# Where dense work stands between attention tiles: a gated linear-attention and ReLU block with split exponentials and a two-step key mask

## The chip, the cores and the metric

The kernel runs on one core of a Trainium2 chip. The metric is the device time of one execution in microseconds (us), as the median of several runs. The core has a matrix engine (PE, with a separate row PEld for its weight loads), a vector engine (DVE), an activation engine (ACT), GpSimd (POOL), and DMA queues, of which this kernel uses mostly that of SyncE (SP). Each engine works through its own list in order, and the lists are tied together by semaphores. PE writes its results to PSUM, which has eight banks; a bank can be written again only after ACT or DVE has read it.

## The reference, cut to what matters

```python
g = sigmoid((x * gate_w).sum(-1))                    # x: 2048 x 512, bf16
q, k, v = split(x @ wqkv)                            # 32 heads of 16
pq, pk = q @ w_phi, k @ w_phi                        # per head, 16 x 16
phi = concat([softmax(p), softmax(-p)])              # for pq and pk: 32 features
kv = einsum("bhsf,bhsd->bhfd", phi_k, v)             # sum over all 2048 rows
z  = einsum("bhsf->bhf", phi_k)
o  = (phi_q @ kv) / (phi_q . z + 1e-6)
a  = o @ wo
b  = relu(x @ w1) @ w2                               # hidden width 1376
out = g * a + (1 - g) * b
```

Two things follow for the order of work. Nothing of `o` can be computed before `kv` has been summed over all rows. And `relu(x @ w1)`, the dense branch, depends on nothing of the attention, so it can be placed anywhere.

## The kernel before, in words

The 2048 rows are 16 tiles of 128 (index m), and also 4 chunks of 512 (index c). A small planner class keeps a list per engine; `p.op(engine, fn, after, ev)` appends an instruction that waits for the events in `after` and signals `ev`. So the order of the calls is the order on each engine, and it is written out by hand at the end of the program (L477 to L573).

The attention work for tile m:

- `atile(m)` (L302): eight matmuls of 128x480 (L307), alternating between bank 0 (query) and bank 1 (key), give the head projections. Softmax is invariant to a shift, so 15 columns per head are computed and the sixteenth exponential is a constant 1. Then ACT makes two exponentials over both banks together (L318, 128x960 each): `ep`, with scale +1, and `em`, with scale -1. The banks are free for tile m+1 when `em` is done. DVE sums the key exponentials per head (L322, event `zk`), takes the reciprocal (L325, `rz`), sums the query's (L327, `zq`) and takes a reciprocal (L332, `rq`). POOL scales the key features (L334, `pk`), forms the query's factor (L339, `sc`) and scales half of the query features (L341, `pq`). A DMA transposes the query features into PHQ (L346, `tq`).
- `vtile(m)` (L350): four matmuls for the values in bank 2 (L354), copied out by ACT (L364).
- `kv(m)` (L367): eight matmuls of 128x65 (L376) that add the tile to the sums in banks 6 and 7; it waits for `pk` of tile m.
- `kvfin` (L382), after the last `kv`: DVE masks the sums to the block diagonal, one bank at a time: L385 and L389 for bank 6 (event `kvz0`), then for bank 7 (`kvz1`).
- `nd(m)` (L404): eight matmuls of 128x68 (L408) with KVNZ give numerator and denominator for tile m, four into each of two banks; even tiles use banks 0 and 1, odd ones 2 and 3. DVE takes the reciprocal (L414) and multiplies (L418, `om`), and a DMA transposes the result.

The dense branch: a *dense unit* `hunit(c, k)` (L254) is four matmuls of 128x512 (L257) in one of the banks 3 to 5 in rotation, and a ReLU on ACT (L243). A *ragged unit* `rest(c)` (L264) is sixteen narrow matmuls (L269) for the last 96 columns of the hidden width and the gate's column; ACT then makes a ReLU (L276) and the gate's exponential (L278). `finB(m)` (L429, matmuls at L433) is the second dense matmul of a tile, `finA(m)` (L440, L442) the output projection of the attention, and `comb(m)` (L452) mixes them (L456) and stores them. `gate()` (L397) is three small DVE instructions (L398, L400, L401) that turn the gate's exponentials into g and 1 - g.

The middle of the program is the loop over m at L523: `atile(m)`, `kv(m - 3)` from m = 3 on, `vtile(m + 3)` up to m = 12, and then units from the list `mid` (L511), dealt by a formula (L529). The formula gives:

```
m      0 1 2 | 3 4 5 6    7 8 9 10 11 12   13   14 15
dense  2 2 2 | 1 2 1 1    2 1 2 1  2  1    0    2  2
ragged       |       1                1    1
```

What stands on PE between `atile(m)` and `atile(m+1)` is called the *filler* below. After the loop come `gate()`, and the six units (3, 4) to (3, 9) of the list `late`, two after each of `kv(13)`, `kv(14)` and `kv(15)`; `kvfin` is queued on DVE after `kv(15)` (L542 to L551). Then `nd(0)`, `finB(0)`, `nd(1)` and the loop at L556. It runs `finB(1)`, `nd(2)`, `nd(3)`, `finA(0)` for m = 0, and then `nd(m + 3)`, `finB(m + 1)`, `finA(m)` for each further m.

Of the kernel before, what the change touches and what calls it, by code (L numbers as in the profile page):

```python
# [5 lines left out]
ACT = mybir.ActivationFunctionType  # L6
# [51 lines left out]
def bass_gated_mix__linear_kernel_hedgehog__dense_activation_relu__prompt_kernel(  # L58
# [13 lines left out]
    S, D = x2.shape  # L72
    H = A_w_phi.shape[0]
    DH = A_w_phi.shape[1]
    DFF = B_w1.shape[1]
    P = 128
    NT = S // P
    NDT = D // P
# [4 lines left out]
    NG = 8  # L83
    HG = H // NG
    FE = DH - 1
    DE = H * FE
    GW = 128
    NB = 5
    VB = 6
    LAG = 3  # L90
    KU = KT - 1
    NR = DFF - KU * P

    with ExitStack() as es:
        E = es.enter_context
        XT = E(nc.sbuf_tensor("XT", [P, NDT, S], BF16))
# [4 lines left out]
        WQK = E(nc.sbuf_tensor("WQK", [P, 2, NDT * D], BF16))  # L101
# [4 lines left out]
        EB = E(nc.sbuf_tensor("EB", [P, NB, 4, 2 * D], BF16))  # L106
# [22 lines left out]
        PS = E(nc.psum_tensor("PS", [P, 8, 512], FP32))  # L129
# [6 lines left out]
        EBS = NB * 4 * 2 * D  # L136
# [62 lines left out]
        def xready(c):  # L199
            return ["xa0", "xa1", "xa2", "xb1", "xb2"] if c == 0 else [f"x{c}"]  # L200
# [84 lines left out]
        def pre(i):  # L285
# [13 lines left out]
                     after=[f"pm{i}"], ev=f"pc{i}")  # L299
            free[bank] = [f"pc{i}"]  # L300

        def atile(m):  # L302
            b = m % NB
            first = xready(m // 4) + free[0] + free[1] + ([f"pc{i}" for i in range(8)] if m == 0 else [])
            for dt in range(NDT):
                for which in range(2):
                    p.op("pe", lambda e, dt=dt, which=which: e.matmul(  # L307
                        PS[:, which, 0:DE], XT[:, dt, m * P:(m + 1) * P], WQK[:, which, dt * DE:(dt + 1) * DE],
                        start=(dt == 0), stop=(dt == NDT - 1)),
                        after=(first if dt == 0 and which == 0 else ()),  # L310
                        ev=(f"qk{m}" if dt == NDT - 1 and which == 1 else None))
            src = PS[:, 0:2, 0:DE].rearrange("p a (h f) -> p a h f", h=H)
            base = b * 8 * D
            dsts = (bass.AP(tensor=EB, offset=base, ap=[[EBS, P], [4 * D, 2], [32, H], [1, FE]]),
                    bass.AP(tensor=EB, offset=base + 2 * D + 16, ap=[[EBS, P], [2 * D, 2], [32, H], [1, FE]]))
            busy = [f"tq{m - NB}", f"pk{m - NB}", f"pq{m - NB}"] if m >= NB else []
            for s, nm in ((0, "ep"), (1, "em")):
                p.op("act", lambda e, s=s, o=dsts[s]: e.activation(  # L318
                    o, src, ACT.Exp, scale=(1.0 if s == 0 else -1.0)),
                    after=[f"qk{m}"] + busy, ev=f"{nm}{m}")  # L320
            free[0] = free[1] = [f"em{m}"]
            p.op("dve", lambda e: e.tensor_reduce(  # L322
                ZB[:, b, 64:128], EB[:, b, 2, :].rearrange("p (g f) -> p g f", f=DH), AX.X, ALU.add),
                after=[f"em{m}", f"cst{b}"], ev=f"zk{m}")
            p.op("dve", lambda e: e.reciprocal(SC[:, b, 64:128], ZB[:, b, 64:128]),  # L325
                 after=[f"zk{m}"] + ([f"pk{m - NB}"] if m >= NB else []), ev=f"rz{m}")
            p.op("dve", lambda e: e.tensor_reduce(  # L327
                ZB[:, b, 0:64].rearrange("p (h s) -> p h s", s=2),
                bass.AP(tensor=EB, offset=base, ap=[[EBS, P], [32, H], [2 * D + 16, 2], [1, DH]]), AX.X, ALU.add),
                after=([f"sc{m - NB}"] if m >= NB else []), ev=f"zq{m}")  # L330
            zq = ZB[:, b, 0:64].rearrange("p (h s) -> p h s", s=2)
            p.op("dve", lambda e: e.reciprocal(SC[:, b, 32:64], zq[:, :, 1]),  # L332
                 after=[f"zq{m}"] + ([f"sc{m - NB}"] if m >= NB else []), ev=f"rq{m}")
            p.op("pool", lambda e: e.tensor_tensor(  # L334
                EB[:, b, 3, :].rearrange("p (g f) -> p g f", f=DH),
                EB[:, b, 2, :].rearrange("p (g f) -> p g f", f=DH),
                SC[:, b, 64:128].unsqueeze(2).to_broadcast([P, 2 * H, DH]), ALU.mult),
                after=[f"rz{m}"] + ([f"kv{m - NB}"] if m >= NB else []), ev=f"pk{m}")
            p.op("pool", lambda e: e.tensor_tensor(SC[:, b, 0:32], zq[:, :, 0], SC[:, b, 32:64], ALU.mult),  # L339
                 after=[f"rq{m}"], ev=f"sc{m}")  # L340
            p.op("pool", lambda e: e.tensor_tensor(  # L341
                EB[:, b, 0, :].rearrange("p (h s f) -> p h s f", h=H, s=2)[:, :, 1, :],
                EB[:, b, 1, :].rearrange("p (h s f) -> p h s f", h=H, s=2)[:, :, 1, :],
                SC[:, b, 0:32].unsqueeze(2).to_broadcast([P, H, DH]), ALU.mult),
                after=[f"sc{m}"] + ([f"tq{m - NB}"] if m >= NB else []), ev=f"pq{m}")
            p.dma("sp", lambda e: e.dma_start_transpose(  # L346
                out=PHQ[:, :, m * P:(m + 1) * P], in_=EB[:, b, 0, :]),
                f"tq{b}", after=[f"pq{m}", f"cst{b}"] + (["pm7"] if m == 12 else []), ev=f"tq{m}")
# [54 lines left out]

        def nd(m):  # L404
            b0 = 2 * (m % 2)
            after = [f"tq{m}", "kvz1"] + free[b0] + free[b0 + 1]
            for g in range(NG):
                p.op("pe", lambda e, g=g: e.matmul(  # L408
                    PS[:, b0 + g // 4, (g % 4) * GW:(g % 4) * GW + 68],
                    PHQ[:, g, m * P:(m + 1) * P], KVNZ[:, g, :], start=True, stop=True),  # L410
                    after=(after if g == 0 else ()), ev=(f"nd{m}" if g == NG - 1 else None))
            r = m % 2
            ob = m % 3
            p.op("dve", lambda e: e.reciprocal(  # L414
                RDEN[:, r, :].rearrange("p (g h) -> p g h", g=NG),
                bass.AP(tensor=PS, offset=b0 * 512 + 64, ap=[[EPS, P], [GW, NG], [1, HG]])),
                after=[f"nd{m}"], ev=f"rd{m}")
            p.op("dve", lambda e: e.tensor_tensor(  # L418
                OTM[:, ob, :].rearrange("p (g h d) -> p g h d", g=NG, h=HG),
                bass.AP(tensor=PS, offset=b0 * 512, ap=[[EPS, P], [GW, NG], [DH, HG], [1, DH]]),  # L420
                bass.AP(tensor=RDEN, offset=r * H, ap=[[2 * H, P], [HG, NG], [1, HG], [0, DH]]), ALU.mult),
                after=[f"rd{m}"] + ([f"to{m - 3}"] if m >= 3 else []), ev=f"om{m}")
            free[b0] = free[b0 + 1] = [f"om{m}"]
            p.dma("sp", lambda e: e.dma_start_transpose(
                out=OT[:, :, m * P:(m + 1) * P], in_=OTM[:, ob, :]), f"to{ob}", after=[f"om{m}"], ev=f"to{m}")
# [82 lines left out]
        for i in range(4, 8):  # L508
            pre(i)
        vtile(2, "dve")  # L510
        mid = [(1, k) for k in range(KU)] + [(1, -1)] + [(2, k) for k in range(KU)] + [(2, -1), (3, -1)]  # L511
        last = [(3, k) for k in range(KU)]
        mid += last[:4]
        late = last[4:]

        def unit(c, k):
            if k < 0:
                rest(c)
            else:
                hunit(c, k)  # L520

        done = 0
        for m in range(NT):  # L523
            atile(m)
            if m >= LAG:
                kv(m - LAG)
            if m + 3 < NT:
                vtile(m + 3)
            while done < (2 * (m + 1) if m < 3 else 6 + ((m - 2) * (len(mid) - 6)) // (NT - 3)):  # L529
                unit(*mid[done])  # L530
                done += 1
            if m == 3:
                for i in range(2):
                    a, b = (0, 6) if i == 0 else (6, KU)
                    p.dma("sp", lambda e, a=a, b=b: e.dma_start(
                        out=W2[:, a:b, :], in_=B_w2[a * P:b * P, :].rearrange("(j p) n -> p j n", p=P)),
                        "w2", ev=f"w2{i}")
                p.dma("sp", lambda e: e.dma_start(out=W2[0:NR, KU, :], in_=B_w2[KU * P:DFF, :]), "w2", ev="w2")
            if m == 5:
                p.dma("sp", lambda e: e.dma_start(  # L540
                    out=WO[:, :, :], in_=A_wo.rearrange("(j p) n -> p j n", p=P)), "wo", ev="wo")
# [12 lines left out]
        nd(1)  # L554
        FB = (4, 5, 7)
        for m in range(NT):  # L556
            if m > 0 and m + 3 < NT:
                nd(m + 3)
            if m + 1 < NT - 1:
                finB(m + 1, FB[(m + 1) % 3])  # L560
            if m == 0:
                nd(2)
                nd(3)
            finA(m, (6, 2, 0)[max(m - NT + 3, 0)])
            if m < NT - 1:
                comb(m)
        m = NT - 1
# [59 lines left out]
```

## Time and profile before

| what | value |
|---|---|
| median of 7 runs | 152.62 us (152.45 to 153.53) |
| the profiled execution: its own time | 152.75 us |
| its span, first to last instruction | 150.8 us |
| PE busy | 145.5 us (96%) in 996 matmuls |
| DVE, ACT, POOL busy | 93.1, 71.4, 53.9 us |
| granted PE clock | 1.00 |

The span is 1.95 us shorter than the profiled execution's own time. It has three stages: loads and the first dense chunk up to 20.5 us, the loop over attention tiles with the late units up to 91.7 us, and the loop of `nd`, `finB` and `finA` to the end.

Three views of the profile are used. The *timeline* has instructions in order of time, with start and duration. The *chain* is the work that ended last, followed back from the end: each line has a start, a length, an engine, a tensor and a source line; "issue" is time in which nothing is shown as waited for. A *group row* has one source line's count, its busy time and the mean length of one in ns, and the idle time before it. A matmul is shown with its full length (366 ns for L307), though the next one starts before it ends, so for PE the distance between starts is what counts.

### The profile page before, as it was taken

The page shows a single profiled execution, that of the slowest core. Times are in us where ns is not written, and L with a number is a line of the kernel's source. Part 1 is how long each engine was busy: PE and PEld are TensorE (multiplying, and loading weights), DVE is VectorE, ACT ScalarE, POOL GpSimd, SP SyncE. Part 2 cuts the span into 40 slices and gives each one's busy share as a digit, 9 for nine tenths or more (in the row PEclk, how much of TensorE's full clock was granted, in tenths as well). Part 3 has the DMA queues.
Part 4 walks back from the last instruction along what each step waited for, and adds up shares of the span by engine and source line. Part 5 has one row for each costly group of instructions (what it writes and reads, how often), then busy time and mean ns, then how long its engine had stood idle before and what let it go on. Part 6 is the DMA issues. An engine that isn't in the chain of part 4 may idle for free.

```text
span 150.8 us, 2557 instructions
## 1 busy us (share of the span) xinstructions
PE 145.5 (96%) x996; PEld 74.0 (49%) x996; DVE 93.1 (62%) x154; ACT 71.4 (47%) x111; POOL 53.9 (36%) x63
## 2 busy tenths in 40 slices
PE   7899999999999999999979999999999999999992
PEld 2574744444546444444544544544544444444452
DVE  2427765777868787868678895484444455555232
ACT  3306338887777777778867763011122211111150
POOL 2040000788786876868787880000000000000000
PEclk9999999999999999999999999999999999999999
DMA  4999983034349969032634453334323332222312
GB/s 156 314 283 210 166 180 82 0 74 70 70 83 310 161 125 223 17 74 57 70 70 104 104 74 70 70 70 107 72 72 85 84 75 71 70 70 70 83 63 70
DMA packets 44516, 16.11 MB, mean 107 GB/s; under 512 B 39288, under 2 KB 43736, under 8 KB 44504
## 3 DMA queue, kind: packets, MB, share of 16 engines
q1 hardware_dynamic: 44352, 15.92, 50.4%
q8 instruction: 8, 0.13, 0.5%
q10 hardware_dynamic: 152, 0.03, 0.1%
q14 instruction: 4, 0.03, 0.1%
HBM read 4.41 MB, written 2.10 MB: 43 GB/s over the span
## 4 chain that ended last, share of the span: by engine, by line
PE 84%; DVE 7%; DMA 3%; ACT 2%; issue 1%; SPq 1%
PE PS L433 25%; PE PS L307 18%; PE PS L257 14%; PE PS L442 9%; PE PS L354 9%; PE PS L471 4%; DMA W<-in_B_w_dram 3%; PE PS L408 3%; ACT EB L318 2%; PE PS L376 2%; PE PS L269 1%; DVE ZB L322 1%; DVE WQK L296 1%; DVE ZB L327 1%; DVE OMG L401 1%
## 5 line engine op out<-in xcount | busy, mean ns | idle before, releaser
L433 PE MATMUL PS<-W,HT 128*128 128x512 bf16 (+4 forms) x187 | 40.6, 366 | 0.0
L334 POOL TENSOR_TENSOR EB<-EB,SC 128x1024 bf16<-128x1024 bf16 x16 | 30.8, 1928 | 27.3 <-DVE SC L325 27.3
L318 ACT ACTIVATE EB<-PS 128x960 bf16<-128x960 f32 x32 | 29.3, 970 | 17.1 <-PE PS L307 17.1
L447 ACT ACTIVATE TFA<-PS,GT 128x512 bf16<-128x512 f32 x16 | 11.0, 687 | 43.3 <-PE PS L442 36.9
L257 PE MATMUL PS<-XT,W 128*128 128x512 bf16 x128 | 30.7, 379 | 0.0
L307 PE MATMUL PS<-WQK,XT 128*128 128x480 bf16 x128 | 28.6, 367 | 1.1 <-ACT EB L318 1.0
L322 DVE TENSOR_REDUCE ZB<-EB 128x64 f32<-128x1024 bf16 x16 | 19.5, 1220 | 15.3 <-ACT EB L318 15.3
L456 DVE SCALAR_TENSOR_TENSOR WQK<-PS,OMG,TFA 128x512 bf16<-128x512 f32 (+2 forms) x17 | 12.2, 719 | 25.0 <-ACT TFA L447 23.8
L433 PEld LDWEIGHTS PS<-W,HT 128*128 128x128 bf16 (+1 forms) x187 | 17.0, 98 | 17.1
L243 ACT ACTIVATE HT<-PS 128x512 bf16<-128x512 f32 x35 | 20.3, 610 | 7.3 <-PE PS L471 4.7
L307 PEld LDWEIGHTS PS<-WQK,XT 128*128 128x128 bf16 x128 | 11.9, 98 | 15.9 <-ACT EB L318 3.4
L257 PEld LDWEIGHTS PS<-XT,W 128*128 128x128 bf16 x128 | 12.1, 98 | 13.7
L327 DVE TENSOR_REDUCE ZB<-EB 128x64 f32<-128x1024 bf16 x16 | 18.6, 1161 | 0.0
L341 POOL TENSOR_TENSOR EB<-EB,SC 128x512 bf16<-128x512 bf16 x16 | 16.9, 1055 | 1.3
L354 PE MATMUL PS<-WV,XT 128*128 128x512 bf16 x64 | 16.4, 379 | 0.0
L442 PE MATMUL PS<-WO,OT 128*128 128x512 bf16 x64 | 16.1, 378 | 0.0
L418 DVE TENSOR_TENSOR WQK<-PS,RDEN 128x512 bf16<-128x512 f32 x16 | 11.1, 691 | 0.6
L442 PEld LDWEIGHTS PS<-WO,OT 128*128 128x128 bf16 x64 | 6.2, 97 | 7.4
L325 DVE RECIPROCAL SC<-ZB 128x64 f32<-128x64 f32 x16 | 8.8, 553 | 0.5
L408 PEld LDWEIGHTS PS<-KVNZ,PHQ 128*128 128x128 bf16 x128 | 5.9, 97 | 4.3 <-issue 1.2
L414 DVE RECIPROCAL RDEN<-PS 128x32 f32<-128x32 f32 x16 | 5.6, 349 | 3.7 <-PE PS L408 3.7
L364 ACT ACTIVATE VS<-PS 128x512 bf16<-128x512 f32 x13 | 7.9, 605 | 0.0
(54 smaller groups left out, 89.9 us busy)
## 6 DMA issues: line engine op xcount, KB each, us to landing
out_dram<-WQK SPq DMA_DIRECT2D x15, 128.0 KB, 1.7
W<-in_B_w_dram SPq DMA_DIRECT2D x4, 344.0 KB, 5.2
W<-in_B_w_dram SPq DMA_DIRECT2D x1, 768.0 KB, 5.0
OT<-in_A_x_dram SPq DMA_DIRECT2D x2, 256.0 KB, 3.6
WV<-in_A_wqkv_dram SPq DMA_DIRECT2D x1, 512.0 KB, 6.7
W<-in_B_w_dram SPq DMA_DIRECT2D x1, 512.0 KB, 6.1
WO<-in_A_wo_dram SPq DMA_DIRECT2D x1, 512.0 KB, 6.5
PHQ<-EB SPq DMA_TRANSPOSE x16, 2.8
```

Source lines behind the costliest of these rows:

```text
L243: p.op("act", lambda e: e.activation(dst, src, ACT.Relu), after=[f"h{c}_{kt}"], ev=ev)
L257: p.op("pe", lambda e, t=t: e.matmul(PS[:, bank, :], W1[:, t, kt * P:(kt + 1) * P], XT[:, t, c * 512:(c + 1) * 512], start=(t == 0), stop= ...
L307: p.op("pe", lambda e, dt=dt, which=which: e.matmul(PS[:, which, 0:DE], XT[:, dt, m * P:(m + 1) * P], WQK[:, which, dt * DE:(dt + 1) * DE] ...
L318: p.op("act", lambda e, s=s, o=dsts[s]: e.activation(o, src, ACT.Exp, scale=(1.0 if s == 0 else -1.0)), after=[f"qk{m}"] + busy, ev=f"{nm} ...
L322: p.op("dve", lambda e: e.tensor_reduce(ZB[:, b, 64:128], EB[:, b, 2, :].rearrange("p (g f) -> p g f", f=DH), AX.X, ALU.add), after=[f"em{ ...
L327: p.op("dve", lambda e: e.tensor_reduce(ZB[:, b, 0:64].rearrange("p (h s) -> p h s", s=2), bass.AP(tensor=EB, offset=base, ap=[[EBS, P], [ ...
L334: p.op("pool", lambda e: e.tensor_tensor(EB[:, b, 3, :].rearrange("p (g f) -> p g f", f=DH), EB[:, b, 2, :].rearrange("p (g f) -> p g f", ...
L341: p.op("pool", lambda e: e.tensor_tensor(EB[:, b, 0, :].rearrange("p (h s f) -> p h s f", h=H, s=2)[:, :, 1, :], EB[:, b, 1, :].rearrange( ...
L354: p.op("pe", lambda e, dt=dt: e.matmul(PS[:, bank, :], XT[:, dt, m * P:(m + 1) * P], WV[:, dt, :], start=(dt == 0), stop=(dt == NDT - 1)), ...
L433: p.op("pe", lambda e, kt=kt, M=M: e.matmul(PS[:, bank, 0:n], HT[0:M, kt, m * P:(m + 1) * P], W2[0:M, kt, cs], start=(kt == 0), stop=(kt = ...
L442: p.op("pe", lambda e, t=t: e.matmul(PS[:, bank, :], OT[:, t, m * P:(m + 1) * P], WO[:, t, :], start=(t == 0), stop=(t == NDT - 1)), after ...
L456: p.op("dve", lambda e: e.scalar_tensor_tensor(out=OSB[:, ob, cs], in0=PS[:, bank, 0:n], scalar=OMG[:, m:m + 1], in1=TFA[:, m % 2, cs], op ...
```

## The change

It has four parts.

1. Units are dealt by a written list per tile instead of by the formula. The total up to m = 15 stays 27, and `late` stays the same six units:

```
m      0 1 2 3 4 5* 6 7 8* 9 10 11* 12 13* 14* 15*
dense  2 2 2 2 2 1  1 2 1  1 2  1   1  2   2   0
ragged              1      1        1
```

2. In the six tiles with a star, the two exponentials of 128x960 become four of 128x480: `ep` and `em` of the key bank first, then of the query bank. The key sum L322 waits for the key's `em` alone, and the query sum L327 for the last. In the tile after a starred one, the eight projection matmuls run four for the key bank and then four for the query bank; the first of each four waits for its own bank.
3. In `nd`, the first matmul waits for `kvz0` and the fifth for `kvz1`.
4. `nd(4)` moves from ahead of `finB(2)` to behind it.

```diff
+        split = (5, 8, 11, 13, 14, 15)
+
         def atile(m):
             b = m % NB
-            first = xready(m // 4) + free[0] + free[1] + ([f"pc{i}" for i in range(8)] if m == 0 else [])
...
+            first = xready(m // 4) + ([f"pc{i}" for i in range(8)] if m == 0 else [])
+            order = [(dt, w) for dt in range(NDT) for w in range(2)]
+            if m - 1 in split:
+                order = [(dt, w) for w in (1, 0) for dt in range(NDT)]
+            for i, (dt, which) in enumerate(order):
+                p.op("pe", lambda e, dt=dt, which=which: e.matmul(
...
+                    after=(first if i == 0 else []) + (free[which] if dt == 0 else []),
+                    ev=(f"qk{m}" if i == 7 else None))
...
+            if m in split:
+                for w, nm in ((1, "k"), (0, "")):
+                    expo(0, w, f"ep{nm}{m}")
+                    expo(1, w, f"em{nm}{m}")
+            else:
+                expo(0, None, f"ep{m}")
+                expo(1, None, f"em{m}")
+            emk = f"emk{m}" if m in split else f"em{m}"
+            free[1] = [emk]
+            free[0] = [f"em{m}"]
             p.op("dve", lambda e: e.tensor_reduce(
                 ZB[:, b, 64:128], EB[:, b, 2, :].rearrange("p (g f) -> p g f", f=DH), AX.X, ALU.add),
-                after=[f"em{m}", f"cst{b}"], ev=f"zk{m}")
+                after=[emk, f"cst{b}"], ev=f"zk{m}")
...
-                after=([f"sc{m - NB}"] if m >= NB else []), ev=f"zq{m}")
+                after=[f"em{m}"] + ([f"sc{m - NB}"] if m >= NB else []), ev=f"zq{m}")
...
         def nd(m):
             b0 = 2 * (m % 2)
-            after = [f"tq{m}", "kvz1"] + free[b0] + free[b0 + 1]
+            after = [f"tq{m}", "kvz0"] + free[b0] + free[b0 + 1]
...
-                    after=(after if g == 0 else ()), ev=(f"nd{m}" if g == NG - 1 else None))
+                    after=(after if g == 0 else ["kvz1"] if g == 4 else ()), ev=(f"nd{m}" if g == NG - 1 else None))
...
+        mid = [[(1, 0), (1, 1)], [(1, 2), (1, 3)], [(1, 4), (1, 5)], [(1, 6), (1, 7)], [(1, 8), (1, 9)], [(2, 0)],
+               [(1, -1), (2, 1)], [(2, 2), (2, 3)], [(2, 4)], [(2, -1), (2, 5)], [(2, 6), (2, 7)], [(2, 8)],
+               [(3, -1), (2, 9)], [(3, 0), (3, 1)], [(3, 2), (3, 3)], []]
...
-            if m > 0 and m + 3 < NT:
+            if m > 1 and m + 3 < NT:
                 nd(m + 3)
             if m + 1 < NT - 1:
                 finB(m + 1, FB[(m + 1) % 3])
+            if m == 1:
+                nd(m + 3)
             if m == 0:
                 nd(2)
                 nd(3)
```

The new helper `expo(s, w, ev)` issues one exponential with scale +1 or -1 (s), over bank w alone or, with w = None, over both banks.

More of the change, by code (lines that the diff above doesn't have):

```diff
@@ L300, in pre @@
             free[bank] = [f"pc{i}"]
+        split = (5, 8, 11, 13, 14, 15)
         def atile(m):
             b = m % NB
-            first = xready(m // 4) + free[0] + free[1] + ([f"pc{i}" for i in range(8)] if m == 0 else [])
[L305 to L311, printed above, removed]
+            first = xready(m // 4) + ([f"pc{i}" for i in range(8)] if m == 0 else [])
[4 more added lines that the diff above has]
+                p.op("pe", lambda e, dt=dt, which=which: e.matmul(
+                    PS[:, which, 0:DE], XT[:, dt, m * P:(m + 1) * P], WQK[:, which, dt * DE:(dt + 1) * DE],
+                    start=(dt == 0), stop=(dt == NDT - 1)),
+                    after=(first if i == 0 else []) + (free[which] if dt == 0 else []),
+                    ev=(f"qk{m}" if i == 7 else None))
@@ L312, in atile @@
             src = PS[:, 0:2, 0:DE].rearrange("p a (h f) -> p a h f", h=H)
             base = b * 8 * D
-            dsts = (bass.AP(tensor=EB, offset=base, ap=[[EBS, P], [4 * D, 2], [32, H], [1, FE]]),
-                    bass.AP(tensor=EB, offset=base + 2 * D + 16, ap=[[EBS, P], [2 * D, 2], [32, H], [1, FE]]))
             busy = [f"tq{m - NB}", f"pk{m - NB}", f"pq{m - NB}"] if m >= NB else []
[L317 to L320, printed above, removed]
@@ L321, in atile, with expo @@
-            free[0] = free[1] = [f"em{m}"]
+            def expo(s, w, ev):
+                step = (4 * D, 2 * D)[s]
+                off = base + s * (2 * D + 16)
+                scale = (1.0, -1.0)[s]
+                if w is None:
+                    dst = bass.AP(tensor=EB, offset=off, ap=[[EBS, P], [step, 2], [32, H], [1, FE]])
+                    s_ = src
+                else:
+                    dst = bass.AP(tensor=EB, offset=off + w * step, ap=[[EBS, P], [32, H], [1, FE]])
+                    s_ = src[:, w, :, :]
+                p.op("act", lambda e: e.activation(dst, s_, ACT.Exp, scale=scale),
+                     after=[f"qk{m}"] + busy, ev=ev)
@@ L322, in atile @@
+            if m in split:
+                for w, nm in ((1, "k"), (0, "")):
+                    expo(0, w, f"ep{nm}{m}")
+                    expo(1, w, f"em{nm}{m}")
+            else:
+                expo(0, None, f"ep{m}")
[3 more added lines that the diff above has]
+            free[0] = [f"em{m}"]
             p.op("dve", lambda e: e.tensor_reduce(
                 ZB[:, b, 64:128], EB[:, b, 2, :].rearrange("p (g f) -> p g f", f=DH), AX.X, ALU.add),
-                after=[f"em{m}", f"cst{b}"], ev=f"zk{m}")
+                after=[emk, f"cst{b}"], ev=f"zk{m}")
@@ L510, in bass_gated_mix__linear_kernel_hedgehog__dense_activation_relu__prompt_kernel @@
         vtile(2, "dve")
[L511 to L514, printed above, removed]
+        mid = [[(1, 0), (1, 1)], [(1, 2), (1, 3)], [(1, 4), (1, 5)], [(1, 6), (1, 7)], [(1, 8), (1, 9)], [(2, 0)],
+               [(1, -1), (2, 1)], [(2, 2), (2, 3)], [(2, 4)], [(2, -1), (2, 5)], [(2, 6), (2, 7)], [(2, 8)],
+               [(3, -1), (2, 9)], [(3, 0), (3, 1)], [(3, 2), (3, 3)], []]
+        late = [(3, k) for k in range(4, KU)]
         def unit(c, k):
@@ L520, in unit @@
                 hunit(c, k)
-        done = 0
         for m in range(NT):
@@ L528, in bass_gated_mix__linear_kernel_hedgehog__dense_activation_relu__prompt_kernel @@
                 vtile(m + 3)
-            while done < (2 * (m + 1) if m < 3 else 6 + ((m - 2) * (len(mid) - 6)) // (NT - 3)):
-                unit(*mid[done])
-                done += 1
+            for u in mid[m]:
+                unit(*u)
             if m == 3:
```

## The prediction

> **What bounds the kernel now.** I read the page first: busy time by engine, then the rows of the changed lines.
>
> ```profile
> PE 145.5 (96%) x996; PEld 74.0 (49%) x996; DVE 93.1 (62%) x154; ACT 71.4 (47%) x111; POOL 53.9 (36%) x63
> L318 ACT ACTIVATE EB<-PS 128x960 bf16<-128x960 f32 x32 | 29.3, 970 | 17.1 <-PE PS L307 17.1
> L298 ACT ACTIVATE WQK<-PS 128x480 bf16<-128x480 f32 x4 | 2.1, 576 | 0.6 <-PE PS L291 0.6
> ```
>
> PE is the bound at a granted clock of 1.00, and the change removes no PE work. What it can win is PE's idle time. I look for that in the chain, in order of time.
>
> ```profile
> 33.32 1.62 PE PS L307 x8
> 34.94 0.25 PE PS L376 x8
> 35.18 0.86 PE PS L354 x4
> 36.05 0.86 PE PS L257 x4
> 36.91 1.75 PE PS L307 x8
> ...
> 74.60 1.63 PE PS L307 x8
> ...
> 77.12 0.98 ACT EB L318
> 78.10 0.05 issue
> 78.15 1.79 PE PS L307 x8
> ...
> 83.70 1.84 ACT EB L318 x2
> 85.54 0.02 issue
> 85.57 1.23 DVE ZB L322
> 86.80 0.02 issue
> 86.82 0.55 DVE SC L325
> ...
> 89.74 1.02 DVE OMG L401
> ...
> 91.50 0.09 DVE KVNZ L389
> ...
> 91.73 0.41 PE PS L408 x8
> ...
> 97.84 0.70 DVE WQK L418
> 98.55 0.14 issue
> 98.68 0.42 PE PS L408 x8
> ```
>
> The first five lines give the PE prices: projections 1.62, kv 0.25, values 0.86, a dense unit 0.86 (two take 1.73); a ragged one is 0.69 in the same view. Tile 4's projections show 1.75: they waited 0.12 for tile 3's exponentials. The cycle of a tile whose successor waits is 3.71 (timeline starts 33.15 and 36.86). Where the filler is longer than about 2.09, PE doesn't wait.
>
> All stalls from 20.5 us on, by timeline starts less PE prices: tiles 4, 6, 9 and 11, each after one dense unit, 4 x 0.12 = 0.46 (0.115 each); tile 14, after a lone ragged unit, 78.15 - (74.44 + 1.62 + 0.25 + 0.69) = 1.15; tile 15, 0.12. Then nd(0): PE ends its units at 91.42 and starts at 91.73, so 0.31. Then nd(4), waiting for L418 of nd(2): 98.68 - 98.37 = 0.31. Sum 2.35 us. That is all that these edits could take back.
>
> From 83.7 us on the chain is not PE. It goes from tile 15's exponentials through DVE, the gate and the masks to nd(0). The timeline shows what lies beside it:
>
> ```profile
> 87.45 1.93 POOL L334 TENSOR_TENSOR EB<-EB,SC 128x1024 bf16<-128x1024 bf16 x1 [0.45 <-DVE SC L325]
> 89.44 0.42 PE L376 MATMUL PS<-VS,EB 128*128 128x65 bf16 x8
> ```
>
> kv(15) starts 0.06 after POOL's pk(15) ends: PE and POOL arrive together here.
>
> **Part 1, the deal.** Every filler now holds two units, or one dense unit in a tile with split exponentials. With 33.15 as tile 3's start (nothing changes before), full tiles cost 1.62 + 0.25 + 0.86 + 1.73 = 4.46, ragged plus dense 4.29, one unit 3.60, and 3.60 also for tiles 13 and 14 (two units, no values). If no tile waits: tile 4 at 37.61, tile 9 at 58.01, tile 13 at 74.65, tile 14 at 78.24, tile 15 at 81.84. Before, tile 15 started at 81.87. So the 1.73 us of stalls are gone, but tile 15 is not earlier: two dense units of 1.73 us now stand ahead of it instead of behind it. What behind tile 15 can't be shortened by PE work gives that back.
>
> **Part 2, split exponentials.** The nearest row is L298, 480 columns out of PSUM: 576 ns. Two of L318 take 1.83, so their pitch is 0.86, 0.11 under a length. With the same overlap a half has a pitch of 0.466. The key half is done after 0.466 + 0.576 = 1.04 instead of 1.83, and all four after 3 x 0.466 + 0.576 = 1.97, 0.14 more than now. The Trainium skill (ScalarE: Activation LUTs, section "What ACT_TABLE_LOAD costs") speaks against the split: every ACTIVATE pays a fixed 186 ns, of which neighbours overlap 93. By its figures a half takes 586, the key half ends at 1.08 and all four at 2.07 (estimates). I take the row; the rule makes the gain 0.04 less.
>
> Does anything wait in a split tile? ACT starts 1.83 after the tile's projections. The next key projections may start at 1.83 + 1.04 + 0.06 = 2.93, and PE comes at 3.60. The query half comes at 3.60 + 0.81 = 4.41, and its exponentials are done at 1.83 + 1.97 + 0.06 = 3.86. Neither waits; the slack is 0.55. Behind that second wait stand the rest of the projections, kv and all later PE work. The semaphore wait in the middle of the eight costs nothing if satisfied: the waits of the value matmuls, met early, leave the 0.86 pitch without a gap. The upper bound is 0.2 (a weight load of 98 ns not taken ahead and a restart like the 0.12 to 0.15 at waits above), in five tiles ahead of tile 15: 1.0 us. I take zero, nearest to the met waits, and nothing below it, since PE waits for neither half. ACT has room: exponentials 1.97, a copy and a ReLU of 0.6 each in a 3.60 cycle. DVE (1.23 + 0.55 + 1.16 + 0.35) and POOL (1.93 + 0.25 + 1.06) need some 3.3 each, which fits.
>
> **The end of tile 15.** Its key sum starts at 81.84 + 1.83 + 1.04 + 0.04 = 84.75 against 85.57: 0.82 earlier. DVE is free (tile 14's last reciprocal ends near 84.4) and POOL too (pq(14) ends near 86.3, pk(15) starts at 86.63). pk(15) then ends at 88.56, and kv(15) can start at 88.62. PE arrives sooner: 81.84 + 1.62 + kv(12) and kv(13) 0.49 + 1.73 + kv(14) 0.25 + 1.73 = 87.66. It waits **0.96 us**, with two units and nd(0) queued behind. That is where most of the removed stalls go. PE then reaches nd(0) at 88.62 + 0.25 + 1.73 = 90.60.
>
> **Part 3, two-step mask.** The DVE chain from the key sum to nd(0) keeps its length of 91.73 - 85.57 = 6.16: kvz1 lets matmul five go at 84.75 + 6.16 = 90.91. kvz0 lies 0.43 ahead, 90.48. So nd(0) starts at 90.60, its second half waits until 90.91 (it would come at 90.73), and finB(0) starts at 91.04 against 91.99: **0.95 earlier**, 0.82 from the split and 0.13 from the mask. What is queued behind this wait is finB(0).
>
> **Part 4, nd(4).** Its 0.31 disappears: finB(2) uses bank 7, long free, and by its end, 2.38 later, L418 is done. nd(4)'s transpose keeps its place in SP's queue (after the first output, before the second), and finA(4), which needs it, is about three cycles of 3.50 later. Nothing new is late: nd(5) uses the other banks. If that cover were gone, the 0.31 would be back.
>
> Sum: 0.95 + 0.31 = 1.26 us, a little over half of 2.35; the rest is the 0.96 at kv(15) and 0.18 inside nd(0). The profiled execution would go from 152.75 to 151.49 (span 149.54, and 1.95 around it). The median shown is 0.13 below that execution, so 152.62 - 1.26 = **151.36**.
>
> **The rivals.**
>
> *Nothing is given back.* If pk(15) were ready when PE comes, nd(0) would start at 87.66 + 0.25 + 1.73 = 89.64: 2.09 + 0.31 = 2.40 won, 150.2. For it: PE has the work. Against: the DVE chain of 6.16 that starts no earlier than 84.75. 5%.
>
> *The split doesn't do what it says.* If the key sum starts no earlier than after all four exponentials, the chain behind tile 15 is 0.14 longer than now: 0.13 + 0.03 + 0.31 - 0.14 = 0.33 won, 152.3. With the waits in mid-group at their upper bound the gain is 1.26 - 1.0 = 0.26, 152.4. Between these and the forecast lie partial cases. The runs before add to this: three of seven are above 153.4 and four below 152.7, so a median can land high by itself. For these together: no 128x480 exponential and no wait inside a group are in the trace. 25%.
>
> *Slower: the query half comes late.* If short exponentials overlap less, the second wait blocks PE in five successors (tiles 6, 9, 12, 14, 15). With pitch p, each waits 1.83 + 3p + 0.576 + 0.06 - 4.41, and tile 15's key sum is later by p - 0.466. The gain is used up at p = 0.72 and it is 0.5% slower from 0.77. At p = 0.80, near the 0.86 of a full-size one, the five waits are 0.46 each, 2.28, and with 0.33 for the key sum the time is 152.62 - 1.26 + 2.61 = 154.0. Against: L298's row, 576 ns for one alone. 6%.
>
> **How the numbers follow.** Forecast 64%: gain 1.0 to 1.6, 151.0 to 151.6. Larger 5%, smaller or none 25%, slower 6%. A measurement of this kernel tells about 0.5% (0.76 us, 151.86) from no change. The first two cases are faster, 0.69; the smaller gains are within 0.5%, with a little of the slower case, 0.26; slower by more, 0.05. The range runs from 150.4, just short of the full gain, to 152.5, the mid-group bound plus a median that lands high.
>
> **What would show it.** In the profile after: no PE wait on L318 inside the loop and all tile cycles 3.60, 4.29 or 4.46; tile 15 still near 81.8; half exponentials of 576 ns with a pitch near 0.47; pk(15) starting 0.8 earlier and PE waiting 0.9 to 1.0 for POOL ahead of kv(15); finB(0) near 91.0; nd(4) without a wait. I am wrong if the half exponentials have a pitch above 0.6, if the query half's matmuls wait, if tile 15 starts later than 82, or if DVE isn't free at 84.75.

## The result, and the profile after

The changed kernel takes 151.18 us (median of 12 runs, 150.89 to 152.07), the kernel before 152.73 (31 runs, 152.45 to 153.85). The ratio is 0.9893, 95% interval [0.9874, 0.9912]: 1.3 to 1.9 us faster. The forecast was 151.36, so the time lies in the range and on the forecast side; the forecast gain of 1.26 us lies just short of that interval. The profiled execution took 151.37 with a span of 149.6; forecast were 151.49 and 149.54. One run of e8 below, 153.00 at a granted clock of 0.989 where all others have 0.998 to 1.00, was in a slow state and is left out of its median.

First the page of the changed kernel, the engines:

```profile
PE 144.1 (96%) x996; PEld 74.3 (50%) x996; DVE 93.2 (62%) x154; ACT 72.0 (48%) x123; POOL 54.0 (36%) x63
```

ACT has twelve instructions more and 0.6 us more work, PE the same 996 matmuls in a shorter span. (Lines have moved: projections L307 are L311 now, exponentials L318 are L330, the key sum L343, POOL's `pk` L355, kv L397, nd L429, finB L454.) The exponentials, in groups by shape:

```profile
L330 ACT ACTIVATE EB<-PS 128x960 bf16<-128x960 f32 x20 | 18.3, 970 | 10.0 <-PE PS L311 10.0
L330 ACT ACTIVATE EB<-PS 128x480 bf16<-128x480 f32 x24 | 11.8, 578 | 5.4 <-PE PS L311 5.4
```

A half takes 578 ns. The prediction took 576 from a copy of the same width. Next the chain in order of time (start, length, what), around tiles 4, 14 and 15 and the start of the last stage:

```profile
36.17 1.73 PE PS L257 x8
37.89 1.62 PE PS L311 x8
...
76.78 1.73 PE PS L257 x8
78.51 1.62 PE PS L311 x8
...
82.10 1.63 PE PS L311 x8
83.73 0.02 issue
83.76 1.04 ACT EB L330 x2
84.80 0.02 issue
84.83 1.23 DVE ZB L343
86.06 0.02 issue
86.08 0.56 DVE SC L346
86.64 0.07 issue
86.71 1.94 POOL EB L355
88.65 0.05 issue
88.69 0.42 PE PS L397 x8
89.12 1.73 PE PS L257 x8
90.84 0.36 PE PS L429 x8
91.20 2.38 PE PS L454 x11
```

Where the chain before had 1.75 for tile 4's projections, and ACT ahead of tile 14's, there is now 1.62 and nothing but PE. After tile 15 the chain still leaves PE. It goes through two half exponentials (1.04), DVE and POOL to kv(15), and comes back to PE there: `pk(15)`, not the gate, is now the link. The waits of PE itself, from the view of who waited for whom (total, times, longest), show the same: before, there were 1.0 for ACT and 0.2 at nd(4), the first two lines; after, neither, and one new one, the third. (The small waits of 0.12 don't show in this view, only in the starts.)

```profile
PE PS L307 <- ACT EB L318: 1.0, 1, 1.0
PE PS L408 <- DVE WQK L418: 0.2, 1, 0.2
...
PE PS L397 <- POOL EB L355: 0.8, 1, 0.8
```

To compare traces without the loads at the front, I count from the start of tile 0's first matmul to the start of finA(13)'s, by the timeline. The first two lines are from the kernel before, the others from the changed one.

```profile
20.51 1.79 PE L307 MATMUL PS<-WQK,XT 128*128 128x480 bf16 x8
143.02 2.75 PE L442 MATMUL PS<-WO,OT 128*128 128x512 bf16 x12
...
20.63 1.79 PE L311 MATMUL PS<-WQK,XT 128*128 128x480 bf16 x8
141.76 2.75 PE L463 MATMUL PS<-WO,OT 128*128 128x512 bf16 x12
```

That is 143.02 - 20.51 = 122.51 us before and 141.76 - 20.63 = 121.13 after: **1.38 less**.

| stretch, from timeline starts | before | after | difference | forecast |
|---|---|---|---|---|
| tile 0 to tile 15 | 61.36 | 61.31 | -0.05 | -0.03 |
| tile 15 to its key sum | 3.70 | 2.89 | -0.81 | -0.79 |
| its key sum to finB(0) | 6.42 | 6.21 | -0.21 | -0.13 |
| finB(0) to finA(13) | 51.03 | 50.72 | -0.31 | -0.31 |

### The profile page after: what moved, and what is told of

Same layout as the page of the kernel before. It is cut to its first block, busy times and chain, and to the rows that moved or that the text cites. A ratio compares the mean times of both kernels' runs of the same rounds, so it can differ in the third digit from the quotient of the medians.

```text
span 149.6 us, 2575 instructions
## 1 busy us (share of the span) xinstructions
PE 144.1 (96%) x996; PEld 74.3 (50%) x996; DVE 93.2 (62%) x154; ACT 72.0 (48%) x123; POOL 54.0 (36%) x63
## 4 chain that ended last, share of the span: by engine, by line
PE 88%; DMA 3%; DVE 3%; POOL 1%; SPq 1%; ACT 1%; issue 0%
PE PS L454 25%; PE PS L311 17%; PE PS L257 16%; PE PS L463 9%; PE PS L375 9%; PE PS L492 4%; DMA W<-in_B_w_dram 3%; PE PS L429 3%; PE PS L397 2%; PE PS L269 2%; POOL EB L355 1%; DVE ZB L343 1%; DVE WQK L296 1%; ACT EB L330 1%; DVE WQK L477 1%; PE PS L291 1%
## 5 line engine op out<-in xcount | busy, mean ns | idle before, releaser
L454 PE MATMUL PS<-W,HT 128*128 128x512 bf16 (+4 forms) x187 | 40.6, 366 | 0.0
L355 POOL TENSOR_TENSOR EB<-EB,SC 128x1024 bf16<-128x1024 bf16 x16 | 30.9, 1929 | 26.3 <-DVE SC L346 26.3
L330 ACT ACTIVATE EB<-PS 128x480 bf16<-128x480 f32 (+1 forms) x44 | 30.1, 756 | 15.4 <-PE PS L311 15.4
L311 PE MATMUL PS<-WQK,XT 128*128 128x480 bf16 x128 | 28.5, 366 | 0.1
L343 DVE TENSOR_REDUCE ZB<-EB 128x64 f32<-128x1024 bf16 x16 | 19.5, 1220 | 14.5 <-ACT EB L330 14.5
L454 PEld LDWEIGHTS PS<-W,HT 128*128 128x128 bf16 (+1 forms) x187 | 17.1, 98 | 17.4
L311 PEld LDWEIGHTS PS<-WQK,XT 128*128 128x128 bf16 x128 | 12.4, 98 | 14.2 <-DVE WQK L296 0.6
L492 PE MATMUL PS<-XT,W 128*128 128x256 bf16 (+1 forms) x48 | 7.3, 308 | 1.2 <-DMA W<-in_B_w_dram 0.9
L397 PEld LDWEIGHTS PS<-VS,EB 128*128 128x128 bf16 x128 | 5.9, 97 | 4.2 <-POOL EB L355 1.3
```

The costliest lines, as they stand in the source:

```text
L311: p.op("pe", lambda e, dt=dt, which=which: e.matmul(PS[:, which, 0:DE], XT[:, dt, m * P:(m + 1) * P], WQK[:, which, dt * DE:(dt + 1) * DE] ...
L330: p.op("act", lambda e: e.activation(dst, s_, ACT.Exp, scale=scale), after=[f"qk{m}"] + busy, ev=ev)
L343: p.op("dve", lambda e: e.tensor_reduce(ZB[:, b, 64:128], EB[:, b, 2, :].rearrange("p (g f) -> p g f", f=DH), AX.X, ALU.add), after=[emk, ...
L355: p.op("pool", lambda e: e.tensor_tensor(EB[:, b, 3, :].rearrange("p (g f) -> p g f", f=DH), EB[:, b, 2, :].rearrange("p (g f) -> p g f", ...
L454: p.op("pe", lambda e, kt=kt, M=M: e.matmul(PS[:, bank, 0:n], HT[0:M, kt, m * P:(m + 1) * P], W2[0:M, kt, cs], start=(kt == 0), stop=(kt = ...
```

## The experiments

Two theories stood after this. The *chain theory*: the waits removed inside the loop (1.73 us) bring nothing by themselves, because two dense units went from behind tile 15 to ahead of it, and what follows tile 15 is a chain through ACT, DVE and POOL; the gain is the split in tile 15, the mask and nd(4). The *deal theory*: the fuller fillers make the gain. All results first; "tile 15" and "finA(13)" are starts counted from tile 0's start in the profiled run, and a ratio is to the kernel before, run beside it (medians 152.62 for e1 to e4, 152.46 for e5 to e7, 153.00 for e8 to e10).

| kernel | tile 15 | finA(13) | median us | ratio, 95% interval |
|---|---|---|---|---|
| before | 61.36 | 122.51 | 152.73 | 1 |
| changed | 61.31 | 121.13 | 151.18 | 0.9893 [0.9874, 0.9912] |
| e1 deal only | 61.93 | 123.07 | 153.22 | 1.0044 [1.0030, 1.0059] |
| e2 formula's deal | 60.31 | 120.80 | 150.75 | 0.9870 [0.9851, 0.9889] |
| e3 nd(4) back | 61.30 | 121.44 | 151.21 | 0.9912 [0.9890, 0.9934] |
| e4 tile 15 not split | 61.31 | 121.93 | 151.94 | 0.9958 [0.9942, 0.9974] |
| e5 full fillers | 59.58 | 120.07 | 150.60 | 0.9878 [0.9847, 0.9909] |
| e6 one-step mask | 61.31 | 121.32 | 151.32 | 0.9930 [0.9907, 0.9953] |
| e7 gate behind masks | 61.30 | 121.02 | 151.03 | 0.9912 [0.9884, 0.9939] |
| e8 = e5 again | 59.58 | 120.07 | 150.49 | 0.9852 [0.9811, 0.9893] |
| e9 = e5, no split | 60.62 | 121.25 | 151.81 | 0.9917 [0.9885, 0.9948] |
| e10 = e5, all split | 59.58 | 120.08 | 150.63 | 0.9842 [0.9804, 0.9881] |

Differences of 0.1 to 0.3 us (e3, e6, e7) rest on one trace each; the medians don't resolve them. That the stretch repeats is seen where it was taken twice: e5 and e8 are the same kernel and both have 120.07.

**e1: the deal alone**, on the kernel before.

```diff
-        mid = [(1, k) for k in range(KU)] + [(1, -1)] + ...
+        mid = [[(1, 0), (1, 1)], ... , [(3, 2), (3, 3)], []]
...
-            while done < (...):
+            for u in mid[m]:
```

> The kernel before with the written deal alone (no split exponentials, old mask wait, old place of nd(4)). Theory (what follows tile 15 is a chain through ACT, DVE and POOL that PE work can't shorten): tiles 6, 9, 12, 14 and 15 each wait 0.12 for the exponentials, so tile 15 starts near 82.4, kv(15) waits about 1.9 for POOL, and finB(0) starts near 92.6 against 91.99; about 0.6 us slower than before. Rival (the waits that the deal removes inside the loop are won): 1.73 - 0.60 = 1.1 us faster than before.

Measured: slower, by 0.44% [0.30, 0.59], and by 0.56 in the trace. PE's timeline (start, length, engine, line, operation) from tile 15 on, with the wait in brackets:

```profile
82.46 1.79 PE L307 MATMUL PS<-WQK,XT 128*128 128x480 bf16 x8
...
90.02 0.42 PE L376 MATMUL PS<-VS,EB 128*128 128x65 bf16 x8 [1.57 <-POOL EB L334]
...
92.57 2.54 PE L433 MATMUL PS<-W,HT 128*128 128x512 bf16 x11
```

Tile 15 starts at 82.46 (82.4 expected), finB(0) at 92.57 (92.6). The deal removes the 1.15 us at tile 14, and all of it and more comes back as one wait for POOL ahead of kv(15). The deal theory is out: by itself the deal loses time.

**e2: the changed kernel with the formula's deal** (the same lines, the other way round).

> The changed kernel with the formula's deal put back, all else kept. Theory (the split and the chain behind tile 15 make the gain, and the deal moves two dense units to the wrong side of tile 15): tile 15 starts near 80.9, one us earlier than in the changed kernel, kv(15) finds POOL done and does not wait, finB(0) starts near 90.7 against 91.04: 0.4 us faster than the changed kernel, 150.8. Rival (the deal makes the gain): tile 14 waits again for about 0.5 us after the lone ragged unit and tiles 4 and 11 for 0.12 each, so some 0.5 to 0.7 us slower than the changed kernel, 151.8.

Measured: 150.75, and 0.33 less than the changed kernel in the trace. The view of the waits shows one in the loop; the timeline shows where it is, and that nothing waits at kv(15) and nd(0):

```profile
PE PS L311 <- ACT EB L330: 0.2, 1, 0.2
```

```profile
76.92 1.91 PE L311 MATMUL PS<-WQK,XT 128*128 128x480 bf16 x8 [0.19 <-ACT EB L330]
...
88.18 0.41 PE L397 MATMUL PS<-VS,EB 128*128 128x65 bf16 x8
88.43 1.89 PE L257 MATMUL PS<-XT,W 128*128 128x512 bf16 x8
90.15 0.42 PE L429 MATMUL PS<-KVNZ,PHQ 128*128 128x68 bf16 x8
90.41 2.54 PE L454 MATMUL PS<-W,HT 128*128 128x512 bf16 x11
```

kv(15), its two units, nd(0) and finB(0) stand at PE prices (0.25, 1.72, 0.26). So with the other parts in, the written deal *costs* 0.33 us. A lone ragged unit in tile 13 is covered for the larger part by tile 13's split: the cycles of tiles 13 and 14 sum to 6.64, against 7.43 before and 6.16 at PE prices. By starts some waits are left in the loop: 0.12 each at tiles 4, 11 and 15, and 0.36 at tile 14. Tile 15 is still 1.00 earlier than in the changed kernel: 1.73 for the two units now behind it, less 0.72 for these waits.

**e3: nd(4) back ahead of finB(2).**

```diff
-            if m > 1 and m + 3 < NT:
+            if m > 0 and m + 3 < NT:
                 nd(m + 3)
...
-            if m == 1:
-                nd(m + 3)
```

> The changed kernel with nd(4) back ahead of finB(2). Theory: nd(4) waits again for L418's multiply of nd(2), 0.31 us, and nothing later absorbs it: 0.3 slower than the changed kernel, 151.5. Rival: a later wait takes it up, no difference.

In the trace finA(13) is 0.31 later than in the changed kernel, and up to finB(0) nothing differs (70.41 in both). The wait is back in its old size:

```profile
97.23 0.41 PE L429 MATMUL PS<-KVNZ,PHQ 128*128 128x68 bf16 x8 [0.15 <-DVE WQK L439]
```

(The bracket counts PE's idle time from a matmul's end; start to start it is the 0.31.) The medians don't resolve it: 151.21 against 151.18, with ratios 0.19% apart in overlapping intervals. The time missed the expected 151.5; the stretch in the trace met it.

**e4: full-size exponentials in tile 15 only.**

```diff
-        split = (5, 8, 11, 13, 14, 15)
+        split = (5, 8, 11, 13, 14)
```

> The changed kernel with full-size exponentials in tile 15 only. Theory: tile 15 starts at the same time, its key sum 0.8 later, kv(15) waits about 1.6 instead of 0.8, finB(0) near 91.8: 0.8 us slower than the changed kernel, 152.0. Rival (the six splits are worth alike, as relief for the next tile's projections): tile 15 has no next tile, so no difference.

Measured: 0.80 later in the trace, 151.94. The wait ahead of kv(15) is 1.58 instead of 0.78:

```profile
89.82 0.42 PE L397 MATMUL PS<-VS,EB 128*128 128x65 bf16 x8 [1.58 <-POOL EB L355]
```

Tile 15 has no projections behind it, so this is the chain's shortening and no relief for PE. Of the six splits this one alone carries 0.8. The other five were not taken out by themselves; the comparison with e1 (tile 15 at 61.31 against 61.93) puts 0.62 on them. So the parts sum up: +0.56 for the deal, -0.62 for five splits, -0.80 for the sixth, -0.19 for the mask (e6) and -0.31 for nd(4) (e3) make -1.36, against -1.38 measured.

**e5: full fillers with two units kept behind tile 15.** If the chain can't be shortened by PE work, a deal should move tile 15 forward and leave units behind it as cover.

```diff
-        split = (5, 8, 11, 13, 14, 15)
+        split = (3, 5, 8, 10, 12, 13, 14, 15)
...
+        mid = [[(1, 0), (1, 1)], [(1, 2), (1, 3)], [(1, 4), (1, 5)], [(1, 6)], [(1, 7), (1, 8)], [(1, 9)],
+               [(1, -1), (2, 0)], [(2, 1), (2, 2)], [(2, 3)], [(2, -1), (2, 4)], [(2, 5)], [(2, 6), (2, 7)], [(2, 8)],
+               [(3, -1), (2, 9)], [(3, 0), (3, 1)], [(3, 2), (3, 3)]]
```

> The changed kernel with another deal: two dense units stay behind tile 15 as in the kernel before; every tile that has one dense unit, or one dense and the ragged one in tile 13, has split exponentials (3, 5, 8, 10, 12, 13, 14, 15). Theory (only PE work that stands behind tile 15 can cover the chain there, so the deal should move tile 15 forward instead): no wait in the loop, tile 15 starts 1.7 us earlier than in the changed kernel, kv(15) and nd(0) don't wait, finB(0) 1.0 us earlier: 150.1 to 150.2, the 2.4 us that all waits of the kernel before add up to. Rival (DVE and POOL, with 3.3 us of work per tile, can't follow cycles of 3.42 to 3.60 so often): kv or the chain behind tile 15 is late by some tenths, 150.7, like the kernel with the formula's deal.

In the trace this is 1.06 less than the changed kernel and 2.44 less than before; 2.35 was the sum of all waits. No wait of PE is left behind the front, and the end of tile 15 reads:

```profile
81.13 1.78 PE L311 MATMUL PS<-WQK,XT 128*128 128x480 bf16 x8
...
88.67 0.41 PE L397 MATMUL PS<-VS,EB 128*128 128x65 bf16 x8
88.92 1.89 PE L257 MATMUL PS<-XT,W 128*128 128x512 bf16 x8
90.65 0.42 PE L429 MATMUL PS<-KVNZ,PHQ 128*128 128x68 bf16 x8
90.91 2.54 PE L454 MATMUL PS<-W,HT 128*128 128x512 bf16 x11
```

From tile 15 to finB(0) is 9.78 here and 9.10 in the changed kernel: longer, since the two units (1.73) stand where waits of about 1.03 were, and all of it PE's. The median, 150.60, is above the 150.2 expected and close to the rival's 150.7, but the wait that the rival needs isn't in the trace. The profiled run says why it is slow itself: tile 0 starts at 21.55 instead of 20.63, since the weight load that the chain begins with landed late (the last section has the lines). Hence e8.

**e8: the same kernel again.**

> The kernel with full fillers and two units behind tile 15, unchanged, for a second set of runs. Theory (its first six runs, 149.9 to 151.2, are spread by the landing of the first weight load, which came 0.9 later in the profiled run of that kernel than in that of the changed one): from the start of tile 0 to finA(13) the trace again takes 120.1 us, 1.0 less than in the changed kernel, and the median comes to 150.2. Rival (this deal brings its own spread): the stretch between varies too.

The stretch is 120.07 again, so the rival is out; the median, 150.49, is again not 150.2. Of the two profiled runs, one took 151.23 with tile 0 at 21.55, the other 150.49 with tile 0 at 20.68: from tile 0 to the end of the span (149.4 and 148.6) both take 127.9. So the spread lies ahead of tile 0 as far as these two show. That the medians lie high for this reason is argued from them, not shown for the other runs. The kernel before, run beside e8, had a median of 153.00, and 152.46 beside e5, so levels also shift by half a microsecond between batches; against it e5 gains 1.9 us and e8, by its ratio, 2.3.

**e6: nd waits for both masks at its first matmul.**

```diff
-            after = [f"tq{m}", "kvz0"] + free[b0] + free[b0 + 1]
+            after = [f"tq{m}", "kvz1"] + free[b0] + free[b0 + 1]
...
-                    after=(after if g == 0 else ["kvz1"] if g == 4 else ()), ...
+                    after=(after if g == 0 else ()), ...
```

> The changed kernel with nd waiting for both masks at its first matmul. Theory: nd(0) starts when its second half may start now plus the 0.07 that a wait ahead of a group costs more: finB(0) 0.13 to 0.20 us later, 151.3 to 151.4. Rival (the two-step wait is worth the whole 0.43 between the two masks): 151.6.

Measured: 0.19 more in the trace, 151.32. The two-step wait is worth 0.19, not the 0.43 between the masks, since in the changed kernel PE comes to nd(0) at 90.68, only 0.16 ahead of the end of the second one at 90.84.

**e7: the gate behind the masks on DVE** (`gate()` called ahead of `nd(0)` instead of ahead of the late units).

> The changed kernel with the three gate instructions queued on DVE behind the masks instead of ahead of them. Theory (nd(0)'s start is set by kv(15) and the two units behind it on PE, the gate only by its second half): the masks are done near 90.0 instead of 90.8, nd(0)'s second half doesn't wait, finB(0) 0.1 to 0.15 earlier, 151.1. Rival (the gate's 2.2 us lie on the chain in full): finB(0) 0.5 or more earlier, 150.7.

Measured: 0.11 less in the trace, 151.03. Counted from tile 0, the masks are done 0.77 earlier (69.44 against 70.21), yet nd(0) starts no earlier (70.04 and 70.05): PE with kv(15) and two units is the limit there. The 0.11 is the wait inside nd(0).

**e9: e5 without any split.**

```diff
-        split = (3, 5, 8, 10, 12, 13, 14, 15)
+        split = ()
```

> The same kernel with full-size exponentials in all tiles; tiles with one unit stay as they are. Theory: tiles 4, 6, 9, 11, 13 and 15 each wait 0.12, tile 14 waits 0.29, 1.0 in sum, and the chain behind tile 15 is 0.8 longer, about as long as PE's way there: finB(0) 1.1 later than with splits, the time that of the changed kernel, 151.2. Rival (two units behind tile 15 hide all exponentials well enough): 0.3 later at most, 150.5.

Measured: 1.18 more than e5 in the trace (1.1 expected); 151.81 against 150.49 for e8 beside it, and not the 151.2 expected. Tile 15 is 1.04 later from seven waits, so full fillers in this sense need the splits in the tiles with short fillers. Behind tile 15 only 0.14 more is lost:

```profile
81.09 1.79 PE L311 MATMUL PS<-WQK,XT 128*128 128x480 bf16 x8
...
88.66 0.42 PE L397 MATMUL PS<-VS,EB 128*128 128x65 bf16 x8
...
90.65 0.52 PE L429 MATMUL PS<-KVNZ,PHQ 128*128 128x68 bf16 x8
```

kv(15) comes 7.57 after tile 15, as in e5 (7.54), and doesn't wait; the small loss is inside nd(0) (0.52 long instead of 0.42). So the full-size exponentials in tile 15, which cost 0.80 in e4, are covered here by the two units behind it.

**e10: e5 with all tiles split** (`split = tuple(range(NT))`).

> The same kernel with split exponentials in all 16 tiles. Theory: the 0.14 us more on ACT per tile lies beside PE work, tiles with two units have over 1 us of slack; no difference from the kernel with eight splits, 150.2. Rival (each activation's fixed cost is paid in the time[...]): eight more tiles, up to 8 x 0.14 = 1.1 slower.

120.08 in the trace, no difference (median 150.63; the 150.2 expected is missed here too): eight more tiles with 0.14 us more of ACT work each cost nothing where PE's filler is longer than the exponentials.

## Why the prediction was right, point by point

- *The price of a half exponential.* 576 ns taken, 578 measured. Four take 1.96 us (1.97 taken), the key half 1.04. The estimates from the Trainium skill's figures (ScalarE: Activation LUTs, section "What ACT_TABLE_LOAD costs") were 586 ns and 1.08 us; the row was nearer.
- *No waits in the loop.* From tile 3 on the cycles are 3.59 or 3.60, 4.29 and 4.46, each within 0.01 of the forecast. The wait in the middle of the eight projections costs nothing when it is met early; its bound of 0.2 was not needed.
- *Tile 15 no earlier.* -0.03 forecast, -0.05 measured. The two units moved ahead of it ate 1.73 us of removed waits. e1 and e2 show this from both sides.
- *The wait at kv(15).* 0.96 forecast. By starts it is 88.69 - (86.03 + 1.73) = 0.93. This is where the gain went that the sum of waits promised, and e5 shows that it could be had: with two units behind tile 15 the wait is gone and 1.06 more is won.
- *The mask.* Forecast 0.13, measured 0.21 in the stretch from the key sum to finB(0), and 0.19 by e6. The term mis-sized is the release of nd(0)'s second half: I carried over the 0.14 from the mask to a waiting first matmul, and a wait inside the group needs about 0.07. That is an estimate: the mask is done at 90.84, and the fifth matmul, taken at half of nd's 0.26 ahead of finB(0)'s 91.04, starts near 90.91.
- *nd(4).* 0.31 forecast and measured, by the stretch after finB(0) and by e3.
- *Rivals.* A late query half did not occur. That the split does nothing is excluded by e4 and e9. Full recovery needed a different deal.
- *The sum.* The prediction's parts close to within 0.05 only: 1.26 won, 0.96 and 0.18 left are 2.40, not 2.35.

The forecast gain of 1.26 was summed from parts of the stretch between tile 0 and finA(13), and 1.38 is its measure there. Of the 1.55 us between the medians, 1.38 is in this stretch. The other 0.17 is not settled. The tail after finA(13) doesn't have it: 7.78 us before and 7.84 after. What lies outside the span was 1.95 and 1.77 us in the two profiled runs, and the front differs between executions by more than that.

## What to carry to other kernels

Count the waits that an edit removes, then ask what ends after the last of them. If a chain through other engines follows the last tile, work dealt ahead of that tile loses its worth as cover, and the removed waits come back as one. Here the same filler units, dealt so that the last tile comes early and some units stay behind it, with two more tiles split, won 2.44 us of trace instead of 1.38; the medians differ by less, 150.60 and 150.49 against 151.18. And a split pays where something waits for its first half: 0.8 us in the last tile while nothing covered its chain (e4), 1.04 in seven tiles with short fillers together (e9), nothing in eight tiles whose fillers outlast the exponentials (e10).

## What was not expected of the hardware

Moving the gate in e7 changed the length of its instructions. Here they are with POOL's lines beside them, first in the changed kernel, then in e7:

```profile
86.71 1.93 POOL L355 TENSOR_TENSOR EB<-EB,SC 128x1024 bf16<-128x1024 bf16 x1 [0.31 <-DVE SC L346]
88.01 0.66 DVE L419 TENSOR_SCALAR EG<-EG 128x16 f32<-128x16 f32 x1
88.70 0.25 DVE L421 RECIPROCAL GT<-EG 128x16 f32<-128x16 f32 x1
88.93 1.06 POOL L362 TENSOR_TENSOR EB<-EB,SC 128x512 bf16<-128x512 bf16 x1
88.99 1.02 DVE L422 TENSOR_SCALAR OMG<-GT 128x16 f32<-128x16 f32 x1
```

```profile
88.68 1.06 POOL L362 TENSOR_TENSOR EB<-EB,SC 128x512 bf16<-128x512 bf16 x1
89.75 0.17 DVE L419 TENSOR_SCALAR EG<-EG 128x16 f32<-128x16 f32 x1
89.95 0.25 DVE L421 RECIPROCAL GT<-EG 128x16 f32<-128x16 f32 x1
90.24 0.17 DVE L422 TENSOR_SCALAR OMG<-GT 128x16 f32<-128x16 f32 x1
```

The same 16 elements per partition take 0.66 and 1.02 us, or 0.17 each. In the changed kernel POOL runs `pk(15)` until 88.64 and `pq(15)` from 88.93 to 89.99, and the two `tensor_scalar` instructions end at 88.67 and 90.01, each 0.02 to 0.03 after POOL's. In e7 POOL's last instruction ends at 89.74, ahead of both. The Trainium skill (SBUF — State Buffer, section "Who interferes with whom") says that a DVE instruction in a two-port mode and GpSimd lock each other out for the whole of an instruction, and that `tensor_scalar` can enter such a mode. The two ends agree with it; that these two were in that mode no trace here shows. `reciprocal` kept its 0.25 in both. In the kernel before, L401 ended at 90.76 and POOL's `pq(15)` at 90.73, so most of the 1.02 that the chain showed for L401 is explained in the same way.

The second is the front. A weight load stands at the start of the chain in eleven of the twelve profiled runs (not in e3), and with the same code it took between 4.79 and 6.11 us: here its line in the kernel before, in the changed kernel, and in e5.

```profile
2.12 4.98 DMA W<-in_B_w_dram
```

```profile
2.13 5.09 DMA W<-in_B_w_dram
```

```profile
2.12 6.01 DMA W<-in_B_w_dram
```

Tile 0 follows at 20.51, 20.63 and 21.55. Over all twelve profiled runs it starts between 20.13 and 21.64, which is as much as this change is worth: for effects of 0.1 to 0.4 us the stretch behind the loads has to be compared, not the time.
